# A linear-attention and ELU block on one core: the state term on four 64x64 array tiles, states without zero blocks, and a re-ordered schedule

## The chip, the core and the metric

The kernel runs on one core of one Trainium2 chip. The time is the device time of one execution in microseconds (us); the kernel before takes 214.02 us, the median of three runs (213.94 to 214.1). A profile of one execution goes with it. The engines are TensorE (PE; its weight loads are listed apart as PEld), VectorE (DVE), ScalarE (ACT), GpSimd (POOL) and the issuing queue of SyncE (SP).

## The reference

Inputs are q, k, v of shape (4, 8, 768, 64) for batch, heads, positions and head size, one decay `lam` for each head, and two weight matrices. First comes decayed linear attention, block by block, with a state of 64 x 64 for each batch and head:

```python
intra = (qb @ kb.T * Dmask) @ vb            # Dmask[i, j] = lam ** (i - j) for i >= j
inter = (qb * lam_pow) @ kv_state
out[:, :, sl] = intra + inter
kv_state = lam_block * kv_state + (kb * rev_pow).T @ vb
```

The heads are put side by side, so x has 3072 rows (batch x position) of 512. Then two dense layers with an ELU between them:

```python
h = x @ w_in                                # (3072, 512) @ (512, 2048)
g = where(h > 0, h, exp(min(h, 0)) - 1)
return g @ w_out                            # (3072, 2048) @ (2048, 512), float32
```

## The kernel before, in words

**Groups.** A block is 128 positions here. A group g is one block of one batch: g = 4 * block + batch, 24 groups. Groups 0 to 3 are worked on singly, the others in pairs (4:5, 6:7, ... 22:23); all operands of the matmuls are fp16.

**Attention of a group.** Loads of q, k, v are issued on POOL (`emit_load`, line 107) and cast on the way. `T` puts q and k in transposed form, head pairs on 128 partitions: on TensorE for groups 0 to 7 (line 285), by a transposing DMA on SP for the others (`W`, line 270). `S` makes the scores of eight heads (line 304), `att_E` multiplies them by the decay mask on VectorE into `pp` (line 320). `P` adds up the output, transposed (line 340: v times `pp`; line 346: state times q, from the second block on), and one VectorE or ScalarE instruction moves it to `xt` (lines 361 and 363; from group 8 on it also multiplies by the row decay `qs`). `kd` is k times its decay (POOL, line 176); `U` multiplies it with v for the new state (lines 408 and 417); `M` decays the old state into `stt` (line 390 on POOL; line 383 on ScalarE from group 12 on); line 440 on VectorE adds the two.

**State with zero blocks.** The state of a batch is a tile of 128 partitions, four head pairs and 128 columns. The two heads of a pair lie on the diagonal, the other two 64 x 64 blocks are zero (filled at the start, lines 202 and 718). So a state matmul contracts over 128 partitions, half of them zeros, and writes 64 output rows; `P` writes the two halves of the output rows by two matmuls beside each other.

**Burst.** From group 4 on, `B:P4:P5:U4:U5` puts the output of a pair and its two state updates behind each other on TensorE.

**Dense layers.** A unit `1:g:j` (`mm1`, line 674) makes 512 columns of h in one PSUM bank out of two (`psH`); ScalarE then runs exp and relu (lines 680, 681) and VectorE the ELU's last step (`g` or `gg`, line 640), which frees the bank. `2:g:j` (`mm2`, line 699) multiplies four tiles of g by w_out. For the pairs listed in `SEVEN` the second layer takes seven products `7:g:0` to `7:g:6` of half the columns (line 551) in place of eight; it needs sums of g (`P`, `D`, `E`: `fp`, `fd`, `fe`, lines 497 on POOL and 500 on VectorE; `SHARED` says which are on POOL) and of w_out (`wf`, line 517; token `F` on VectorE, `G` on POOL). Corners are put together by ScalarE copies, POOL and VectorE (lines 558 to 605), and stored from SP.

**Order.** Every engine runs its instructions in the order in which the program emits them. That order is written out: `POOL_ORDER` for the loads and early POOL work, `OPEN` for the opening up to unit 1:6:5, and from there one loop that puts after each unit one item of the second layer and the attention steps due there, at the distances of `AT` (units before the pair's first). So in the steady part a pair has the order

```
1:14:0 1:14:1 S16:17 7:12:0 1:14:2 7:12:1 1:14:3 B:P16:P17:U16:U17 W18 7:12:2
1:14:4 7:12:3 1:14:5 W19 Lq20 7:12:4 1:14:6 Lk20 7:12:5 1:14:7 Lv20 7:12:6
```

and the kernel ends with 1:22:7 7:20:6 7:22:0 ... 7:22:6. `BANKS` names PSUM banks for the early steps; `late` is a list of VectorE and ScalarE steps that are emitted one at a time.

Of the kernel before, what the change touches and what calls it, by code (L numbers as in the profile page):

```python
# [15 lines left out]
def kernel(  # L16
# [27 lines left out]
    WI = [2] * 8  # L44
    WO = [2] * 8
    POOL_ORDER = (
        "q1 k0 iota k2 k1 q2 v0 v1 i0 i1 v2 i3 i2 o0 o1 d0 k3 q3 i4 i5 d1 o2 d2 o3 d3 o4 v3 o5 "
        "i6 i7 k4 o7 o6 q4 k6 m4 v4 q6 d5 d4 q8 q10 k8 d6 v6 v8 d7 v10 k10 m6"
# [4 lines left out]
        "z3 z0 z1 Z2 Z1 z2 Z0 T0 T1 S0 S1 T2 P0 P1 S2 1:0:0 U0 1:1:0 P2 1:1:1 1:2:0 2:0:0 "  # L53
        "1:2:1 2:1:0 1:0:1 T3 2:2:0 1:0:2 S3 1:2:2 2:2:1 U1 1:1:2 2:1:1 2:0:1 P3 2:0:2 1:3:0 "
        "2:1:2 1:1:3 M 1:2:3 Z3 2:2:2 1:3:2 U2 1:3:1 2:1:3 1:0:3 T4 T5 2:2:3 1:3:3 S4:5 2:3:0 "
        "2:0:3 2:3:2 U3 F0 B:P4:P5:U4:U5 M 2:3:3 1:4:1 T6 1:4:0 G3 T7 2:3:1 G4 W9 1:4:3 G5 G1 "
        "S6:7 1:4:2 G2 2:5:0 2:4:0 1:4:4 1:4:5 W8 B:P6:P7:U6:U7 1:4:7 1:6:1 2:5:1 2:4:1 G7 "
        "1:4:6 1:6:0 G6 2:4:2 S8:9 1:6:2 1:6:4 2:5:2 2:5:3 W11 1:6:3 1:6:6 B:P8:P9:U8:U9 1:6:7 "
        "2:4:3 1:6:5 W10 L12"
# [4 lines left out]
    DELAY = 0  # L64
    COMB = nc.gpsimd

    SEVEN = (8, 10, 12, 14, 16, 18, 20, 22)
    SHARED = {8: 'D', 10: 'ED', 12: 'ED', 14: 'ED', 16: '', 18: '', 20: '', 22: 'ED'}
    AT = {'L': -19, 'l': 1, 'W': -13, 'T': -5, 'S': -7, 'B': -5}
    BANKS = (  # L70
        "S0=M0,A S1=D,C S2=D,M1 S3=D,B P0=M1 P1=M0 P2=B P3=A U0=B U1=B U2=B U3=M1 T0=M1,D "
        "T1=D,C T2=M0,D T3=B T4=B T5=D T6=M1 T7=D M2=C M3=M0"
# [19 lines left out]

    stp = [
        [cpool.tile([128, 2, NHP, 128], FP16, name=f"st{x}_{i}") for i in range(2)]
# [5 lines left out]
    def emit_load(w, g0):  # L100
        n = size_of[g0]
        c, b = divmod(g0, B)
        x = {"q": q, "k": k, "v": v}[w]
        src = x[b : b + n, :, c * L : (c + 1) * L].rearrange("b h p d -> p (b h) d")
        t = asb.tile([128, n, H, 64], FP16, tag=f"{w}n{n}", name=f"{w}n{g0}", bufs=4)
        {"q": qg, "k": kg, "v": vg}[w][g0] = t
        nc.gpsimd.dma_start(out=t[:].rearrange("p b h d -> p (b h) d"), in_=src)  # L107
# [38 lines left out]
    def emit_wi(i):  # L146
        written.add(("i", i))
        f0 = sum(WI[:i]) * 128
        nc.gpsimd.dma_start(
            out=wi16[i][:],  # L150
            in_=moe_w_in[:, f0 : f0 + WI[i] * 128].rearrange("(k p) f -> p k f", p=128),
        )
# [48 lines left out]
    def zero_st1(b):  # L201
        nc.vector.memset(st[b][1], 0.0)

# [8 lines left out]

    dn = cpool.tile([128, H], FP32, name="dn")
    mask = cpool.tile([128, H, 128], FP32, name="mask")
    qs = cpool.tile([128, NHP, 128], FP32, name="qs")
    ks = cpool.tile([128, H], FP32, name="ks")
# [11 lines left out]
    for hh in range(2):  # L228
        r = slice(hh * 64, (hh + 1) * 64)
        nc.vector.tensor_copy(loglam_p[r, :], loglam[r, hh::2])  # L230
    nc.vector.tensor_scalar_add(pos[:, 2:3], pos[:, 1:2], float(L))

    def emit_qs():
        for hp in range(NHP):
            nc.scalar.activation(
                qs[:, hp, :], row[:], AF.Exp, scale=loglam_p[:, hp : hp + 1]
            )
# [90 lines left out]

    def att_P(g):
        cb, b = divmod(g, B)  # L330
        until(E_done, g)
        if cb > 0:
            until(Y_done, g - B)
        vt = of(vg, g)
        qt, _ = qkT[g]
        po = bank(f"P{g}", 0, [128, NHP, 128], FP32, f"psO{g}")
        R = [slice(0, 64), slice(64, 128)]
        for hp in range(NHP):
            for hh, r in enumerate(R):
                nc.tensor.matmul(  # L340
                    po[r, hp, :], lhsT=vt[:, 2 * hp + hh, :], rhs=Pt[(g, hh)][:, hp, :],
                    start=True, stop=(cb == 0), skip_group_check=True,
                )
            if cb > 0:
                for r in R:
                    nc.tensor.matmul(  # L346
                        po[r, hp, :], lhsT=st[b][cb % 2][:, hp, r], rhs=qt[:, hp, :],
                        start=False, stop=True, skip_group_check=True,
                    )

        def evacuate():
            g0 = GFIRST[g]
            n = GSIZE[g0]
            if g0 not in xg:
                xg[g0] = asb.tile(
                    [128, NHP, n * 128], FP16, tag=f"xt{n}", name=f"xt{g0}",
                    bufs=4 if n == 1 else 2,
                )
            dst = xg[g0][:, :, (g - g0) * 128 : (g - g0 + 1) * 128]
            if g < GPE:  # L360
                nc.scalar.copy(out=dst, in_=po[:])
            else:
                nc.vector.tensor_tensor(out=dst, in0=po[:], in1=qs[:], op=ALU.mult)
            X_done.add(g)

        return [evacuate]

    stt = {}

    def att_M(g):  # L370

        cb, b = divmod(g, B)
        if cb == NCB - 1 or b % 2:
            return
        assert {f"U{g - B}", f"U{g - B + 1}"} <= seen
        until(Y_done, g - B)
        until(Y_done, g - B + 1)
        old = stp[b // 2][cb % 2]
        tmp = asb.tile([128, 2, NHP, 128], FP32, tag="stt", name=f"stt{g}", bufs=2)
        stt[g] = tmp  # L380
        if g >= MACT:
            for hp in range(NHP):
                nc.scalar.activation(
                    tmp[:, :, hp, :], old[:, :, hp, :], AF.Copy, scale=upp[:, hp : hp + 1]
                )
            return
        for hh in range(2):
            r = slice(hh * 64, (hh + 1) * 64)
            for x in range(2):
                nc.gpsimd.tensor_tensor(  # L390
                    out=tmp[r, x, :, r], in0=old[r, x, :, r],
                    in1=upp[r].unsqueeze(2).broadcast_to([64, NHP, 64]), op=ALU.mult,
                )
# [5 lines left out]
    def att_U(g, pu=None):  # L399

        cb, b = divmod(g, B)
        if cb == NCB - 1:
            return []
        vt = of(vg, g)
        if pu is None:
            full = bank(f"U{g}", 0, [128, NHP, 128], FP32, f"psU{g}")
            for hp in range(NHP):
                nc.tensor.matmul(
                    full[:, hp, :].rearrange("p (h e) -> p h e", h=2),
                    lhsT=kds[g][:, 2 * hp : 2 * hp + 2, :],  # L410
                    rhs=vt[:, 2 * hp : 2 * hp + 2, :], start=True, stop=True,
                )
        else:
            for hp in range(NHP):
                for hh in range(2):
                    r = slice(hh * 64, (hh + 1) * 64)
                    nc.tensor.matmul(
                        pu[r, hp, :], lhsT=kds[g][:, 2 * hp + hh, :], rhs=vt[:, 2 * hp + hh, :],
                        start=True, stop=True, skip_group_check=True,
                    )  # L420
        if cb > 0:
            return []
        new = st[b][1]

        def update(hh):
            r = slice(hh * 64, (hh + 1) * 64)
            nc.vector.tensor_copy(new[r, :, r], full[r, :, r])
            if hh == 1:
                Y_done.add(g)

        return [lambda: update(0), lambda: update(1)]

    def updates(g, pu):
# [4 lines left out]
        def update(hh):  # L438
            r = slice(hh * 64, (hh + 1) * 64)
            nc.vector.tensor_tensor(  # L440
                out=new[r, :, :, r], in0=stt[g][r, :, :, r], in1=pu[r], op=ALU.add
            )
            if hh == 1:
                Y_done.update((g, g + 1))

        return [lambda: update(0), lambda: update(1)]

    def burst(*ops):

        us = [int(o[1:]) for o in ops if o[0] == "U" and int(o[1:]) // B < NCB - 1]  # L450
        evs, i = [], 0
        for o in ops:
            if o[0] == "P":
                evs += att_P(int(o[1:]))
# [262 lines left out]
    def zero_st(b):  # L717
        nc.scalar.memzero(st[b][0])

# [8 lines left out]
    def ready(t):  # L728
# [4 lines left out]
        if t[0] == "U" and g < 2 * B:  # L733
            assert f"{'z' if g < B else 'Z'}{g % B}" in seen
# [4 lines left out]
    def run(t):  # L739
# [11 lines left out]
        if w in "PUzZ":  # L751
            ready(t)
        if w == "S":
# [4 lines left out]
            late.pop(0)()  # L758
            late.pop(0)()
# [6 lines left out]
        else:  # L766
            {"T": att_T_pe, "1": mm1, "2": mm2, "Z": zero_st, "z": zero_st1,
             "q": lambda g, e: cast_raw(g, "q", e), "k": lambda g, e: cast_raw(g, "k", e),
             "7": mm2_seven, "F": w_sums, "G": lambda i: w_sums(i, nc.gpsimd), "c": lambda i: (emit_qs, emit_mask, emit_ks)[i](), "W": pool_work,
# [94 lines left out]
```

## Time and profile before

| what | before |
|---|---|
| median of 3 runs | 214.02 us (213.94 to 214.1) |
| the profiled execution's own time | 213.94 us |
| span of its instructions | 212.2 us |
| TensorE busy | 196.6 us (93%) |
| POOL busy | 160.2 us (76%) |
| VectorE busy | 158.7 us (75%) |
| ScalarE busy | 138.0 us (65%) |
| unit matmuls, line 674 | 896, 101.1 us |
| score outputs, line 340 / state terms, line 346 | 192, 12.4 us / 160, 10.0 us |

The span runs from the first to the last instruction; what lies between it and the execution's own time is start and end. Busy times of matmuls overlap, so a count times a mean is more than the array's time: how often matmuls start says more. In a row of the timeline stand start, length, engine, line, operation, output and inputs, shape and count; a bracket tells how long the engine stood idle before and what ended that. In the chain of waits stand start, length and the piece of work.

### The profile page before, as it was taken

What the parts mean: (1) busy time and instruction counts of PE and PEld (TensorE: products, weight loads), DVE (VectorE), ACT (ScalarE), POOL (GpSimd) and SP (SyncE); (2) the same over time, 40 slices, a digit from 0 to 9 for tenths busy, and PEclk for the clock granted to TensorE, in tenths of its full rate; (3) what the DMA queues carried; (4) which work ended last, traced back from release to release, by engine and by line L of the source; (5) the groups of instructions that cost most, each with busy time, mean ns of one, the idle gap of its engine ahead of it and who ended that gap; (6) DMA issues with size and microseconds to landing.
All of it is one profiled execution on the core that took longest, in us unless ns stands there. A gap on an engine that the chain in (4) does not pass through costs nothing.

```text
span 212.2 us, 5654 instructions
## 1 busy us (share of the span) xinstructions
PE 196.6 (93%) x2224; PEld 157.3 (74%) x2224; DVE 158.7 (75%) x294; ACT 138.0 (65%) x277; POOL 160.2 (76%) x187
## 2 busy tenths in 40 slices
PE   0678999999999999999999999999999999999983
PEld 0457775777676776767887887888988878888862
DVE  3864482589965878889979879879989889885522
ACT  4535664874877675867866867867667667577630
POOL 7999699999999999597999999996361201206961
PEclk9999999999999999999999999999999999999999
DMA  8999999999993030999949969979999611011032
GB/s 89 132 163 192 195 188 187 161 181 191 134 180 80 3 99 5 131 165 151 125 92 154 133 83 153 163 50 151 155 81 169 103 52 50 3 51 48 3 118 79
DMA packets 102122, 24.61 MB, mean 116 GB/s; under 512 B 92624, under 2 KB 99280, under 8 KB 102096
## 3 DMA queue, kind: packets, MB, share of 16 engines
q0 software_dynamic: 79760, 13.50, 82.6%
q1 hardware_dynamic: 22336, 10.76, 26.3%
q8 instruction: 17, 0.28, 0.6%
q14 instruction: 9, 0.07, 0.1%
HBM read 27.27 MB, written 6.29 MB: 158 GB/s over the span
## 4 chain that ended last, share of the span: by engine, by line
PE 76%; ACT 7%; DVE 6%; DMA 3%; POOL 3%; issue 2%; ACTq 0%; POOLq 0%; DVEq 0%
PE psH L674 35%; PE psM L551 21%; PE psM L699 12%; DMA wi<-in_moe_w_in_dram 3%; ACT e L680 3%; ACT psH L681 3%; PE psS L304 3%; DVE gg L640 3%; PE psO L340 2%; DVE g L640 2%; PE psO L346 2%; POOL kn L107 1%; PE psT L285 1%; POOL qn L107 1%; POOL vn L107 1%
## 5 line engine op out<-in xcount | busy, mean ns | idle before, releaser
L674 PE MATMUL psH<-xt,wi 128*128 128x256 f16 (+1 forms) x896 | 101.1, 261 | 3.0 <-DVE gg L640 1.4
L674 PEld LDWEIGHTS <-wi 128*128 128x128 f16 x896 | 78.8, 99 | 18.3 <-issue 4.0
L680 ACT ACTIVATE e<-psH 128x512 f32<-128x512 f32 x96 | 57.4, 597 | 47.7 <-PE psH L674 46.6
L681 ACT ACTIVATE psH<-psH 128x512 f32<-128x512 f32 x96 | 56.9, 593 | 0.0
L640 DVE SCALAR_TENSOR_TENSOR gg<-e,psH 128x512 f16<-128x512 f32 x64 | 43.7, 683 | 16.6 <-ACT psH L681 16.3
L640 DVE SCALAR_TENSOR_TENSOR g<-e,psH 128x512 f16<-128x512 f32 x32 | 21.9, 685 | 17.3 <-ACT psH L681 17.1
L320 DVE TENSOR_TENSOR pp<-psS,mask 128x512 f16<-128x512 f32 x48 | 31.4, 683 | 4.2 <-PE psS L304 4.2
L699 PE MATMUL psM<-wo,g 128*128 128x512 f16 x128 | 31.9, 379 | 0.0
L497 POOL TENSOR_TENSOR fd<-gg 128x512 f16<-128x512 f16 x20 | 24.4, 1218 | 0.1
L176 POOL TENSOR_TENSOR kd<-kn,ks 128x512 f16<-128x512 f16 x20 | 21.0, 1054 | 4.3 <-DMA kn<-in_k_dram 4.2
L517 POOL TENSOR_TENSOR wf<-wo 128x256 f16<-128x256 f16 (+1 forms) x28 | 21.1, 794 | 0.2
L497 POOL TENSOR_TENSOR fe<-gg 128x256 f16<-128x256 f16 x16 | 11.8, 735 | 12.1 <-DVE gg L640 12.0
L594 POOL TENSOR_TENSOR t<-m,m 128x256 f32<-128x256 f32 x8 | 5.9, 737 | 18.3 <-ACT m L558 18.3
L699 PEld LDWEIGHTS <-g 128*128 128x128 f16 x128 | 11.7, 98 | 9.6
L551 PE MATMUL psM<-wf,gg 128*128 128x256 f16 x128 | 16.8, 273 | 0.8 <-DVE osb L582 0.5
L551 PE MATMUL psM<-wo,fp 128*128 128x256 f16 x128 | 16.5, 273 | 0.0
L551 PE MATMUL psM<-wf,fd 128*128 128x256 f16 x128 | 16.4, 273 | 0.0
L107 POOL DMA_DIRECT2D qn<-in_q_dram x13 | 14.8, 1136 | 0.9 <-POOLq L848 0.8
L107 POOL DMA_DIRECT2D kn<-in_k_dram x14 | 15.3, 1096 | 0.0
L107 POOL DMA_DIRECT2D vn<-in_v_dram x14 | 15.3, 1098 | 0.0
L500 DVE TENSOR_TENSOR fp<-gg 128x512 f16<-128x512 f16 x32 | 14.6, 455 | 0.6
L551 PEld LDWEIGHTS <-gg 128*128 128x128 f16 x128 | 11.9, 98 | 3.2 <-issue 0.7
(62 smaller groups left out, 249.3 us busy)
## 6 DMA issues: line engine op xcount, KB each, us to landing
out_dram<-osb SPq DMA_DIRECT2D x22, 256.0 KB, 2.7
kn<-in_k_dram POOLq DMA_DIRECT2D x10, 256.0 KB, 6.0
qn<-in_q_dram POOLq DMA_DIRECT2D x10, 256.0 KB, 6.2
vn<-in_v_dram POOLq DMA_DIRECT2D x10, 256.0 KB, 8.7
wi<-in_moe_w_in_dram POOLq DMA_DIRECT2D x8, 256.0 KB, 8.0
wo<-in_moe_w_out_dram POOLq DMA_DIRECT2D x8, 256.0 KB, 9.0
kn<-in_k_dram POOLq DMA_DIRECT2D x4, 128.0 KB, 4.2
vn<-in_v_dram POOLq DMA_DIRECT2D x4, 128.0 KB, 6.4
```

The source lines that it names most:

```text
L107: nc.gpsimd.dma_start(out=t[:].rearrange("p b h d -> p (b h) d"), in_=src)
L176: nc.gpsimd.tensor_tensor(out=kd[:], in0=of(kg, g), in1=ks[:].unsqueeze(2).broadcast_to([128, H, 64]), op=ALU.mult,)
L320: nc.vector.tensor_tensor(out=P[:], in0=pts[hh][:], in1=mask[:, hh::2, :], op=ALU.mult)
L497: nc.gpsimd.tensor_tensor(out=out[:], in0=in0, in1=in1, op=op)
L500: lambda out=out, in0=in0, in1=in1, op=op: nc.vector.tensor_tensor(out=out[:], in0=in0, in1=in1, op=op)
L517: eng.tensor_tensor(out=out, in0=in0, in1=in1, op=op)
L551: nc.tensor.matmul(out, lhsT=lhs, rhs=rhs, start=(s == 0 and m in (3, 4, 1, 7)), stop=(s == NFT // 2 - 1), skip_group_check=True,)
L640: nc.vector.scalar_tensor_tensor(out=g.rearrange("p f c t -> p (f c t)"), in0=e[:], scalar=-1.0, in1=r[:], op0=ALU.add, op1=ALU.min,)
L674: nc.tensor.matmul(pH[:, f * n * 128 : (f + 1) * n * 128], lhsT=wi16[i][:, kk, w * 128 : (w + 1) * 128], rhs=xg[g0][:, kk, :], start=(kk = ...
L680: nc.scalar.activation(e[:], pH[:], AF.Exp)
L681: nc.scalar.activation(pH[:], pH[:], AF.Relu)
L699: nc.tensor.matmul(psM[g][:, cols], lhsT=gts[(g, j * FB + f)], rhs=wo16[i][:, w, cols], start=first and f == 0, stop=end and f == FB - 1, ...
```

## The change

- **State.** A state has no zero blocks any more: 128 partitions (two heads), four head pairs, 64 columns. The zero fills go. `M` and the state update are one instruction for both halves of the partitions.
- **Output of a pair.** For groups from 4 on, `att_P2` works on both groups of a pair. The 16 state matmuls come first, each on a 64 x 64 tile of the array, in rounds of four (two row halves, two column halves); the row half decides the PSUM bank (heads of even and of odd number). The scores' matmuls follow into the same banks. Heads h and h + 4 now share the partitions of `xt`, so its row decay is a new constant `qx` (token `c3`).
- **w_in.** Its rows are loaded to match that order of heads: a load brings 64 partitions and 512 columns in place of 128 partitions and 256, so a tile is complete after two loads.
- **Schedule.** Pair 20 leaves `SEVEN`. On POOL are now P and D for pairs 8 and 16, P and E for 12 and 22, E and D for 10 and 14. `F0` becomes `G0`. `OPEN`, `POOL_ORDER`, some `BANKS` and the distances of `AT` are new: W comes two units later, the loads two units earlier. `DELAY` becomes 1, which in `flush` has the effect that 0 had.

```diff
-    WI = [2] * 8
+    WI = [4] * 4
-    OPEN = (
-        "z3 z0 z1 Z2 Z1 z2 Z0 T0 T1 S0 S1 T2 P0 P1 S2 1:0:0 U0 1:1:0 P2 1:1:1 1:2:0 2:0:0 "
-        "1:2:1 2:1:0 1:0:1 T3 2:2:0 1:0:2 S3 1:2:2 2:2:1 U1 1:1:2 2:1:1 2:0:1 P3 2:0:2 1:3:0 "
-        "2:1:2 1:1:3 M 1:2:3 Z3 2:2:2 1:3:2 U2 1:3:1 2:1:3 1:0:3 T4 T5 2:2:3 1:3:3 S4:5 2:3:0 "
...
+    OPEN = (
+        "T0 S0 T1 T2 S1 P0 S2 P1 1:0:0 1:1:0 U0 P2 1:1:1 U1 1:2:0 2:0:0 1:2:1 2:1:0 1:0:1 T3 "
+        "1:0:2 2:2:0 S3 1:2:2 2:2:1 2:0:1 P3 1:1:2 2:1:1 2:0:2 1:3:0 1:1:3 2:1:2 2:2:2 M 1:2:3 "
+        "1:3:2 U2 2:1:3 1:3:1 T4 T5 1:0:3 2:2:3 1:3:3 c3 S4:5 2:3:0 2:0:3 G0 2:3:2 U3 "
...
-    SEVEN = (8, 10, 12, 14, 16, 18, 20, 22)
-    SHARED = {8: 'D', 10: 'ED', 12: 'ED', 14: 'ED', 16: '', 18: '', 20: '', 22: 'ED'}
-    AT = {'L': -19, 'l': 1, 'W': -13, 'T': -5, 'S': -7, 'B': -5}
+    SEVEN = (8, 10, 12, 14, 16, 18, 22)
+    SHARED = {8: 'PD', 10: 'ED', 12: 'PE', 14: 'ED', 16: 'PD', 18: '', 22: 'PE'}
+    AT = {'L': -21, 'l': 1, 'W': -11, 'T': -7, 'S': -7, 'B': -5}
...
-        [cpool.tile([128, 2, NHP, 128], FP16, name=f"st{x}_{i}") for i in range(2)]
+        [cpool.tile([128, 2, NHP, 64], FP16, name=f"st{x}_{i}") for i in range(2)]
...
-            out=wi16[i][:],
-            in_=moe_w_in[:, f0 : f0 + WI[i] * 128].rearrange("(k p) f -> p k f", p=128),
+            out=wi16[i][hf * 64 : hf * 64 + 64],
+            in_=moe_w_in[r0 : r0 + 256, f0 : f0 + WI[i] * 128].rearrange(
+                "(k p) f -> p k f", p=64
+            ),
...
-                    nc.tensor.matmul(
-                        po[r, hp, :], lhsT=st[b][cb % 2][:, hp, r], rhs=qt[:, hp, :],
-                        start=False, stop=True, skip_group_check=True,
-                    )
+    def att_P2(g):
...
+        po = [bank(f"P{g + e}", 0, [128, 2, 2, 128], FP32, f"psO{g}_{e}") for e in range(2)]
+        for a in range(2):
+            for i in range(2):
+                for c in range(2):
+                    for e in range(2):
+                        nc.tensor.matmul(
+                            po[e][R[c], a, i, :],
+                            lhsT=st[(g + i) % B][cb % 2][R[e], 2 * c + a, :],
+                            rhs=qkT[g + i][0][R[e], 2 * c + a, :],
+                            start=(a + i == 0), stop=False, skip_group_check=True,
+                        )
+        for i in range(2):
+            for h in (0, 4, 1, 5, 2, 6, 3, 7):
+                scores_v(po[h % 2][R[h // 4], h % 4 // 2, i, :], g + i, h, False)
...
-        def update(hh):
-            r = slice(hh * 64, (hh + 1) * 64)
-            nc.vector.tensor_tensor(
-                out=new[r, :, :, r], in0=stt[g][r, :, :, r], in1=pu[r], op=ALU.add
-            )
+        def update():
+            nc.vector.tensor_tensor(out=new[:], in0=stt[g][:], in1=pu[:], op=ALU.add)
```

## The prediction

> **What bounds the kernel now.** I read the page first (engine rows, chain of waits), then the timeline of one steady stretch, then the few places where TensorE stands still.
>
> ```profile
> PE 196.6 (93%) x2224; PEld 157.3 (74%) x2224; DVE 158.7 (75%) x294; ACT 138.0 (65%) x277; POOL 160.2 (76%) x187
> PE 76%; ACT 7%; DVE 6%; DMA 3%; POOL 3%; issue 2%; ACTq 0%; POOLq 0%; DVEq 0%
> ```
>
> TensorE carries 76% of the chain. From about 16 us on it works nearly without a break, so a change is worth what it takes off TensorE's own sequence, plus the few holes it closes. The timeline shows what a burst costs there:
>
> ```profile
> 131.76 1.04 PE L674 MATMUL psH<-xt,wi 128*128 128x256 f16 x8
> 132.72 0.25 PE L340 MATMUL psO<-pp,vn 128*64 128x128 f16 x2
> 132.80 0.22 PE L346 MATMUL psO<-qT,st 128*64 128x128 f16 x2
> ...
> 133.64 0.42 PE L417 MATMUL psU<-vn,kd 128*64 128x64 f16 x16
> 133.99 1.05 PE L551 MATMUL psM<-wo,fp 128*128 128x256 f16 x8
> ```
>
> Blocks of eight 256-column matmuls follow each other every 0.873 us, so one takes 0.109. The eight from 131.76 fill the array until 132.63 and the burst starts at 132.72: 0.09 us lie idle where the tile form goes from 128*128 to 128*64. The burst's 16 score and 16 state matmuls run from 132.72 to 133.64, two at a time (rows of x2): 0.92 us for 16 pairs, the first a little longer, the others 0.056 apart by their starts in the trace. The state updates' eight pairs end near 133.89 and the next block starts at 133.99: again 0.10 for a change of form.
>
> ```profile
> 35.28 0.60 ACT e L680
> 36.40 0.70 DVE g L640
> 37.14 1.05 PE psH L674 x16
> ...
> 78.88 0.67 DVE st L440
> 79.59 0.53 DVE st L440
> 80.31 0.70 DVE g L640
> 81.05 1.03 PE psH L674 x8
> ```
>
> These pieces of the chain are the holes: `mm1` has two banks, and where only one other block stands between a unit's end and the unit after next, TensorE waits for ScalarE's two passes and VectorE's `g`. Before 37.14 the hole is 0.36 us, before 81.05 it is 0.30 (there because two state updates stand before `g` on VectorE). Once in each pair of groups, at its second unit, it is 0.37. The tail has two more:
>
> ```profile
> 201.33 0.93 PE L551 MATMUL psM<-wf,gg 128*128 128x256 f16 x7
> 202.58 0.28 PE L551 MATMUL psM<-wf,gg 128*128 128x256 f16 x1 [0.32 <-DVE gg L640]
> 203.37 1.03 PE L551 MATMUL psM<-wf,gg 128*128 128x256 f16 x8 [0.50 <-DVE osb L582]
> ```
>
> The first product of the last pair waits for the last `gg`; the second then waits 0.68 us (202.58 plus 0.11 to 203.37) for its bank, which the last corner of pair 20 (`osb`, line 582) still holds. The opening, last:
>
> ```profile
> 14.74 1.03 PE L674 MATMUL psH<-xt,wi 128*128 128x128 f16 x8
> 16.08 1.04 PE L674 MATMUL psH<-xt,wi 128*128 128x128 f16 x8 [0.31 <-DMA wi<-in_moe_w_in_dram]
> 17.34 1.88 PE L674 MATMUL psH<-xt,wi 128*128 128x128 f16 x16
> 19.60 1.07 PE L674 MATMUL psH<-xt,wi 128*128 128x128 f16 x16
> ```
>
> `mm1` begins when `w_in` lands: its first half on the first load, its second on the second. Sixteen matmuls take 1.88 us at 17.34 and 1.07 at 19.60: early ones run at half the pace, though the page's clock row reads 9 in every slice.
>
> **The change, part by part**, against the profiled execution: 213.94 us, a span of 212.2 and 1.74 around it, 0.08 below the median of the three runs (214.02).
>
> **State term, -1.29.** Ten bursts (P4:P5 to P22:P23) hold 16 state matmuls each: now eight pairs of 0.056, after it four rounds of four tiles. Nothing in the trace shows four tiles at once. Column halves pair (above), and the scores of line 304 show that row halves pair too: 16 of them take 0.56 us in all (128.57 to 129.13), that is 8 x 0.056 and one change of form. So a round costs between 0.056 and 0.112; I take 0.056, since in a pair the second matmul starts only 3 ns after the first. Saved: 10 x 4 x 0.056 = 2.24. But the states now stand first, in 64*64 form, and the scores follow in 128*64: one more change of form in each burst. Its price is between 0 (the column half stays 64 wide) and the 0.10 of the rows; I take 0.095, the size of every change of form at full pace: 0.95.
>
> The Trainium skill, TensorEngine Tiling (Array Packing), Tiling Modes, says that changing the mode, and not just the tile, drains the array. That speaks against the change: by the rule each burst pays as I have it; without it the gain would be 2.24. The skill's TensorE: Matmul & The Clock Gate, Part 3, lets each further tile add some 4 ns, which by an estimate would take 40 x 2 x 4 ns = 0.3 us off the gain; the trace's pairs repeat at 0.056 with no such growth.
>
> **Pair 20 leaves the seven products, +0.78 on TensorE.** Its two groups take 32 matmuls of 512 columns (line 699, four in 0.862 us): 6.90, in place of 56 of 0.109 = 6.12. In exchange, a `2:20:0` stands between the first two units of pair 22, where the order before has none, and fills the hole of 0.37. And the tail's bank: product 2 of pair 22 needs the bank of `psM21`, freed by one ScalarE copy (0.59) right behind the last unit's two passes, about 1.95 us after that unit ends on TensorE. Product 1 ends 2.23 after it (2:21:3, then the wait for `gg`, which stays). So the 0.68 goes. Next late is the P sum of pair 22, now on POOL (1.22): `gg` ends 2.07 after the unit, the sum at 3.4, and its last two factors are wanted at 3.8. It fits by 0.4; without that cover it costs what it lacks.
>
> **Order and VectorE, -0.66.** In the new order two blocks stand before the unit that waits at 37.14, so 0.36 goes. One state update of 128 partitions (0.68) replaces two of 64 partitions, so `g` at 80.31 comes 0.6 earlier and the 0.30 there goes. The other holes at second units stay. VectorE loses more (the P and E sums that go to POOL, `F0`), but it is not what ends those waits: ScalarE and TensorE are. I count 0.
>
> **Opening, +0.25.** A `w_in` load now holds all columns of four tiles for 64 partitions, so unit 1:0:0 needs both halves and can't start at 14.74. The second is the ninth POOL load in both orders, with the same bytes ahead, so it lands near 16.03 as now. Behind the waiting matmul all of TensorE queues: 1:0:0, 1:1:0, U0. Eight matmuls that ran in the hole move behind it, some 0.8 us at the slow pace; given back are U1 (0.22), now in the hole before 1:2:0, and half of that hole (0.61 now, 0.3). The loads of the next tiles (18.24, 19.55) hold later units in both. Bounds: -0.2 (they land earlier in longer rows) to +1.3, one more load of this size (16.03 less 14.69, where the two land now).
>
> **Without a price.** The zero fills (four on VectorE, 1.1; four on ScalarE, 1.4) lie before 30 us beside the wait for `w_in` or before slack. The new `qx` (four ScalarE passes, 1.3) stands behind 1:3:3; the next unit follows after S4:5, three `mm2` and a burst, 5.5 us; uncovered it costs 1.3. M on ScalarE halves its elements and moves behind 1:g:5, where the `e` of unit 6 waits some 0.6 for it; its `gg` then comes 0.1 after its bank is wanted, which the hole of the second unit behind it takes up. W goes two units later (kd, SP transposes), the loads two earlier; on SP only stores of finished corners stand ahead, and transposes landed 137.19 for scores at 144.07.
>
> Sum: -1.29 + 0.78 - 0.37 - 0.68 - 0.66 + 0.25 = -1.97, so 212.0 for this execution and 212.1 against the median.
>
> **The rivals.**
>
> **VectorE was the hidden cause** of more holes. It loses 20 P and 4 E sums (11 us at 0.455 and 0.478), eight updates (5.4) and `F0` (2.4). The kT copy that S6:7 awaits at 56.36 (hole 0.35) follows a VectorE step. If these and some half of the second-unit holes (7 x 0.37) go too, another 1.2: 210.9. Against it: the units' waits end on ScalarE.
>
> **Tiles don't overlap fourfold.** If rows and columns pair but not both, the 2.24 goes and the extra change of form stays: 214.3. Against: both kinds of pair run freely.
>
> **The opening pays in full**: 1.3, and 0.5 if TensorE's slow pace lasts longer for its later start: 213.6.
>
> **POOL becomes the bound** (the slower side). It is already full in a steady pair:
>
> ```profile
> 127.60:143.10 15.50, 15.29 (x184) 13.22 (x184) 13.05 (x24) 11.53 (x25) 15.01 (x17) 1.00 1.13 121
> ```
>
> 15.01 busy of 15.50 us. Pairs 8 and 16 gain four P sums of 1.22 (pair 16 also its four D), G0 joins (3.2); sixteen small M steps become four (-5). Between 80 and 95.6 POOL has 12.9 now and gets about 17 against 15.4 of TensorE. That backlog of 2 to 3 us stays through pair 16, since each pair brings about as much as TensorE takes. It decides where kd comes after its burst: kd(g+1) would run near 143 plus backlog, the burst is at 148.2; so from 5 us of backlog TensorE waits, every pair. If a POOL pair costs 16.8 (its sums stretch from 1.15 to 1.34 beside VectorE), five pairs bring 7 us on top of the first 2.5, less the slack of 5: 212.1 + 4.5 = 216.6.
>
> **How the numbers follow.** The sum as forecast: 0.53; VectorE 0.15; opening 0.12; no fourfold overlap 0.08; POOL 0.12. The predicted time is 212.1; the forecast alone runs from 211.4 to 213.0 (a change of form at 0 to 0.10 each, rounds of up to 0.07, opening from -0.2). The range goes to 210.9 for VectorE and to 214.3 for no overlap. A measurement here tells 0.2% (0.4 us) from no change. Faster: 0.53 + 0.15 + half of the opening + a quarter of POOL (backlog partly absorbed) = 0.77; same: the overlap case and part of the opening, 0.10; slower: the rest of POOL and of these, 0.13.
>
> **What would show it.** Right: state matmuls start in fours every 0.056, a burst is 0.13 shorter though a gap of 0.09 stands between states and scores; no wait at the second unit of pair 22 and none for `osb` in the tail; first unit near 16.1. Wrong: fours that repeat at 0.11; a pair's period that follows POOL, with PE waiting for kd or for sums; `mm1` starting past 17.

## The result, and the profile after

| what | before | after |
|---|---|---|
| median of the runs shown together | 214.06 us (213.94 to 214.34) | 220.67 us (220.22 to 222.23) |
| ratio of the two | | 1.032 (1.0268 to 1.0371) |
| the profiled execution's own time, span | 213.94, 212.2 us | 220.22, 218.5 us |

The changed kernel is 3.2% slower. Forecast were 212.1 us and a gain. Here and below a median is over all executions of a kernel in its set, while a ratio leaves out those that fell in a slower state, so the two do not always match (e2 and e12 most). The page of the changed kernel, its engine row and the shares of the chain:

```profile
PE 196.8 (90%) x2200; PEld 152.9 (70%) x2200; DVE 155.2 (71%) x253; ACT 136.0 (62%) x275; POOL 168.4 (77%) x188
PE 68%; DVE 12%; issue 6%; ACT 6%; DMA 3%; POOL 3%; DVEq 0%; ACTq 0%; POOLq 0%
```

TensorE does the same amount of work (196.8 us) in a span that is 6.3 us longer; its share of the chain falls from 76 to 68%, and VectorE's doubles. So TensorE now waits, and for VectorE. The waits of TensorE between 80 and 170 us say where, first one row of the kernel before, then two of the changed kernel (engine, line waited for: us in total, times, longest):

```profile
PE psH L674 <- DVE gg L640: 1.0, 5, 0.2
```

```profile
PE psH L718 <- DVE gg L684: 5.8, 10, 1.5
PE psO L358 <- DVE pp L336: 1.6, 3, 1.0
```

Pairs 8 to 16 lie there. From the second unit of one pair to that of the next it takes 15.41, 16.70, 17.61 and 18.69 us, where the kernel before has 15.62 and three times 15.50. Before 80 and behind 165 us the changed kernel is ahead of the kernel before, as forecast, if by less (0.32 and 0.42 for 0.50 and 0.53).

Why `gg` is late is seen one step further back, on VectorE. Its groups of corner sums by form (count | busy us, mean ns), first three of the kernel before, then three of the changed one:

```profile
L500 DVE TENSOR_TENSOR fp<-gg 128x512 f16<-128x512 f16 x32 | 14.6, 455 | 0.6
L500 DVE TENSOR_TENSOR fe<-gg 128x256 f16<-128x256 f16 x16 | 7.7, 478 | 0.0
L500 DVE TENSOR_TENSOR fd<-gg 128x512 f16<-128x512 f16 x12 | 5.0, 416 | 0.0
```

```profile
L544 DVE TENSOR_TENSOR fp<-gg 128x512 f16<-128x512 f16 x12 | 12.6, 1053 | 0.2
L544 DVE TENSOR_TENSOR fe<-gg 128x256 f16<-128x256 f16 x12 | 10.6, 887 | 0.1
L544 DVE TENSOR_TENSOR fd<-gg 128x512 f16<-128x512 f16 x12 | 8.2, 686 | 0.2
```

There are 36 of them instead of 60, and they take 31.4 us instead of 27.3. The same instruction takes 0.42 us (512 columns) or 0.285 (256) where nothing disturbs it. Here is one that is disturbed, in the timelines of VectorE, GpSimd and TensorE of the changed kernel (start, us, what):

```profile
137.34 0.68 DVE L403 TENSOR_TENSOR xt<-psO,qx 128x512 f16<-128x512 f32 x1
137.94 2.72 DVE L544 TENSOR_TENSOR fp<-gg 128x512 f16<-128x512 f16 x1
140.58 0.68 DVE L482 TENSOR_TENSOR st<-stt,psU 128x512 f16<-128x512 f32 x1
141.18 1.27 DVE L684 SCALAR_TENSOR_TENSOR gg<-e,psH 128x512 f16<-128x512 f32 x2
```

```profile
136.68 1.20 POOL L109 DMA_DIRECT2D qn<-in_q_dram  x1
137.90 0.68 POOL L541 TENSOR_TENSOR fe<-gg 128x256 f16<-128x256 f16 x1
138.53 1.16 POOL L541 TENSOR_TENSOR fd<-gg 128x512 f16<-128x512 f16 x1
139.64 0.72 POOL L649 TENSOR_TENSOR u<-t,osb 128x256 f32<-128x256 f32 x1
140.31 1.18 POOL L109 DMA_DIRECT2D kn<-in_k_dram  x1
```

```profile
139.72 1.04 PE L595 MATMUL psM<-wf,fe 128*128 128x256 f16 x8
141.91 1.03 PE L718 MATMUL psH<-xt,wi 128*128 128x256 f16 x8 [1.14 <-DVE gg L684]
```

GpSimd has issued the load of q until 137.88 and then starts `fe` at 137.90, 0.04 us ahead of VectorE's `fp`. VectorE's sum stands while `fe`, `fd` and `u` follow each other on GpSimd without a pause, and ends some 0.3 us after `u`. Below, such a sum is called held. Behind it on VectorE wait a state update and `gg`; `gg` frees the psH bank, so TensorE stands for 1.31 us at 140.6 (1.14 of them named in the row).

The kernel before has the same meeting, but it stays short, in its timelines of VectorE and GpSimd:

```profile
131.61 0.58 DVE L500 TENSOR_TENSOR fp<-gg 128x512 f16<-128x512 f16 x1
132.11 0.68 DVE L320 TENSOR_TENSOR pp<-psS,mask 128x512 f16<-128x512 f32 x1
```

```profile
131.24 0.67 POOL L497 TENSOR_TENSOR fe<-gg 128x256 f16<-128x256 f16 x1 [0.39 <-DVE gg L640]
131.87 1.34 POOL L497 TENSOR_TENSOR fd<-gg 128x512 f16<-128x512 f16 x1
```

There `fe` is 0.37 us ahead, VectorE's sum gets its turn when `fe` ends, and GpSimd's `fd` is the one that is stretched (1.34 for 1.16).

### The profile page after: what moved, and what is told of

The parts are those of the page before. It is cut to its first block, busy times and chain, and to the rows that moved or that the text cites. A ratio compares the mean times of both kernels' runs of the same rounds, so it can differ in the third digit from the quotient of the medians.

```text
span 218.5 us, 5560 instructions
## 1 busy us (share of the span) xinstructions
PE 196.8 (90%) x2200; PEld 152.9 (70%) x2200; DVE 155.2 (71%) x253; ACT 136.0 (62%) x275; POOL 168.4 (77%) x188
## 4 chain that ended last, share of the span: by engine, by line
PE 68%; DVE 12%; issue 6%; ACT 6%; DMA 3%; POOL 3%; DVEq 0%; ACTq 0%; POOLq 0%
PE psH L718 32%; PE psM L595 15%; PE psM L743 13%; DVE gg L684 5%; DMA wi<-in_moe_w_in_dram 3%; PE psO L358 3%; ACT psH L725 2%; DVE pp L336 2%; ACT e L724 2%; PE psS L320 2%; DVE fe L544 2%; POOL kn L109 1%; PE psO L388 1%; PE psU L459 1%; POOL qn L109 1%
## 5 line engine op out<-in xcount | busy, mean ns | idle before, releaser
L684 DVE SCALAR_TENSOR_TENSOR gg<-e,psH 128x512 f16<-128x512 f32 x56 | 38.0, 681 | 18.7 <-ACT psH L725 18.6
L684 DVE SCALAR_TENSOR_TENSOR g<-e,psH 128x512 f16<-128x512 f32 x40 | 27.4, 685 | 25.1 <-ACT psH L725 23.4
L743 PE MATMUL psM<-wo,g 128*128 128x512 f16 x160 | 40.1, 379 | 0.0
L541 POOL TENSOR_TENSOR fp<-gg 128x512 f16<-128x512 f16 x16 | 19.7, 1233 | 18.6 <-DVE gg L684 18.5
L561 POOL TENSOR_TENSOR wf<-wo 128x256 f16<-128x256 f16 (+1 forms) x32 | 24.1, 786 | 0.0
L743 PEld LDWEIGHTS <-g 128*128 128x128 f16 x160 | 14.9, 98 | 12.0 <-issue 0.3
L541 POOL TENSOR_TENSOR fd<-gg 128x512 f16<-128x512 f16 x16 | 19.1, 1195 | 0.0
L595 PE MATMUL psM<-wf,gg 128*128 128x256 f16 x112 | 14.6, 273 | 0.3 <-DVE gg L684 0.3
L595 PE MATMUL psM<-wo,fp 128*128 128x256 f16 x112 | 14.4, 273 | 0.0
L544 DVE TENSOR_TENSOR fp<-gg 128x512 f16<-128x512 f16 x12 | 12.6, 1053 | 0.2
```

The costliest lines, as they stand in the source:

```text
L541: nc.gpsimd.tensor_tensor(out=out[:], in0=in0, in1=in1, op=op)
L544: lambda out=out, in0=in0, in1=in1, op=op: nc.vector.tensor_tensor(out=out[:], in0=in0, in1=in1, op=op)
L561: eng.tensor_tensor(out=out, in0=in0, in1=in1, op=op)
L595: nc.tensor.matmul(out, lhsT=lhs, rhs=rhs, start=(s == 0 and m in (3, 4, 1, 7)), stop=(s == NFT // 2 - 1), skip_group_check=True,)
L684: nc.vector.scalar_tensor_tensor(out=g.rearrange("p f c t -> p (f c t)"), in0=e[:], scalar=-1.0, in1=r[:], op0=ALU.add, op1=ALU.min,)
L743: nc.tensor.matmul(psM[g][:, cols], lhsT=gts[(g, j * FB + f)], rhs=wo16[i][:, w, cols], start=first and f == 0, stop=end and f == FB - 1, ...
```

## The experiments

Three theories stood at the start: A, GpSimd has more sums (`SHARED`); B, the new distances (`AT`) put GpSimd's work beside VectorE's sums; C, the new burst, state term or bank. In the table, "lost" is worked out from the starts in each trace: the sum of TensorE's pauses of more than 0.4 us between 80 and 170 us, counted beyond the slot of the matmul ahead. The last column is span less lost.

| kernel | median us | ratio to before (interval) | span | lost (pauses) | rest |
|---|---|---|---|---|---|
| before | 214.06 | | 212.2 | 0 | 212.2 |
| changed | 220.67 | 1.032 (1.027 to 1.037) | 218.5 | 7.6 (8) | 210.9 |
| e1 sums back | 221.24 | 1.034 (1.031 to 1.038) | 219.6 | 8.5 (8) | 211.1 |
| e2 distances back | 215.61 | 1.005 (1.001 to 1.009) | 213.7 | 1.9 (1) | 211.8 |
| e3 before, new sums | 215.94 | 1.011 (1.006 to 1.016) | 215.6 | 2.9 (1) | 212.7 |
| e4 before, new distances | 219.69 | 1.028 (1.024 to 1.033) | 217.8 | 5.3 (5) | 212.5 |
| e5 loads back | 215.72 | 1.009 (1.004 to 1.014) | 214.0 | 3.3 (3) | 210.7 |
| e6 W back | 221.55 | 1.038 (1.031 to 1.044) | 219.9 | 8.8 (7) | 211.1 |
| e7 distances and sums back | 216.91 | 1.017 (1.013 to 1.021) | 215.3 | 3.9 (2) | 211.4 |
| e8 no VectorE sums | 212.39 | 0.993 (0.991 to 0.996) | 210.5 | 0 | 210.5 |
| e9 GpSimd fills | 212.21 | 0.993 (0.989 to 0.996) | 210.2 | 0 | 210.2 |
| e13 e2 with G1 early | 214.24 | 1.003 (0.999 to 1.007) | 212.0 | 1.8 (1) | 210.2 |
| e18 e13, pair 8 on VectorE | 212.38 | 0.994 (0.990 to 0.997) | 210.3 | 0 | 210.3 |

Each ratio is against the runs of the kernel before in the same set (medians 213.28 to 214.06). In all kernels of the table that carry the changed burst the rest stays between 210.2 and 211.8 us, whatever the time; the same holds for e11 (210.6), e14 and e16 (210.4) and e17 (210.2) below, not for e12 (212.8) and e15 (213.0). The forecast's sum gave a span of 212.2 - 1.97 = 210.2.

What e12 and e15 lose beside their pauses is clock. In their traces the granted clock is 0.5 for 3.41 us, from 107.1 and from 124.1 us on, close behind pauses of 2.0 and 2.5 us; a matmul of 256 columns then takes 0.213 us in place of 0.109 (an estimate from that: 1.7 us lost). In e15's timeline of TensorE the blocks of eight that start there stand 1.7 us apart:

```profile
124.21 1.89 PE L602 MATMUL psM<-wo,fp 128*128 128x256 f16 x8
125.89 1.83 PE L725 MATMUL psH<-xt,wi 128*128 128x256 f16 x8
127.56 1.04 PE L602 MATMUL psM<-wo,fp 128*128 128x256 f16 x8
```

The trace of e3 has the same from 103.6 us on, in its pause of 2.9. A mean granted clock of 0.993 or less, which such a stretch makes, stands in all six executions of e15 and in none of the 42 of e8, e9, e10 and e18, whose traces have none of the pauses counted here. What sets it off is not shown: the traces of e6, e7 and e17 have pauses of 2.0 to 2.4 us without it.

### Undoing one part, and doing one part alone (e1 to e4)

```diff
# e1: changed kernel              # e3: kernel before, the reverse
-SHARED = {8: 'PD', 10: 'ED', 12: 'PE', 14: 'ED', 16: 'PD', 18: '', 22: 'PE'}
+SHARED = {8: 'D', 10: 'ED', 12: 'ED', 14: 'ED', 16: '', 18: '', 22: 'ED'}
# e2: changed kernel              # e4: kernel before, the reverse
-AT = {'L': -21, 'l': 1, 'W': -11, 'T': -7, 'S': -7, 'B': -5}
+AT = {'L': -19, 'l': 1, 'W': -13, 'T': -5, 'S': -7, 'B': -5}
```

> The changed kernel with the old split of the sums between POOL and VectorE (P on VectorE again in pairs 8, 12, 16, 22; D on POOL in 8 and 12, E and D in 22, none in 16); all else as changed. Theory A (POOL gets more sums, so VectorE's own sums are held up by POOL's operations, and the units behind them wait): 212 to 213.5 us, VectorE's sums back at 0.42 to 0.6 us. Theory B (the new distances of the loads, of kd and W put POOL work beside VectorE's sums): 217 to 219. Theory C (the new burst or the bank it fills is at fault): 220.

> The changed kernel with the old distances (loads at -19, W at -13); the split of the sums as changed. Theory A: 218 to 221 us, sums on VectorE still above 0.8 us each. Theory B: 212 to 214. Theory C: 220.

> The kernel before with the new split of the sums (P and D on POOL in pairs 8 and 16, P and E in 12 and 22; pair 20 keeps its seven products and its sums on VectorE), all else as before. Theory A: 218 to 221 us. Theory B: 214 to 215. Theory C: 214.

> The kernel before with the new distances (loads at -21, W at -11), all else as before. Theory A: 214 to 214.5 us. Theory B: 217 to 219, with VectorE's sums near 1 us. Theory C: 214.

The distances account for most: taking them back saves 5.1 us (220.67 to 215.61), putting them into the kernel before costs 5.9 (219.69, against 213.83 for the kernel before in the same set). The times of e1, e2 and e4 lie above the ranges that B gave (e1: 221.24 for 217 to 219; e4: 219.69 for 217 to 219; e2: 215.61 for 212 to 214), and what e2 keeps is not from the distances. The sums alone cost the kernel before 2.1, in one pause of 2.9 us behind a sum of 3.89 us; taking them back out of the changed kernel saves nothing. C falls: the old kernel with the new distances loses its time in the same way, and without the new burst.

### Loads or W (e5, e6), and both parts back (e7)

```diff
# e5
-AT = {'L': -21, 'l': 1, 'W': -11, ...
+AT = {'L': -19, 'l': 1, 'W': -11, ...
# e6
+AT = {'L': -21, 'l': 1, 'W': -13, ...
# e7: SHARED as in e1 and AT as in e2 together
```

> Changed kernel with only the loads of the next pair (L, the q, k and v transfers that GpSimd and SyncE issue) put back to their place of before; the W step stays two units later. Theory B1 (the q transfer's issue on GpSimd at unit 2 delays its sums so that they start together with VectorE's): the 2.7 us sum in the middle of each pair (the one at 137.94 us in the changed kernel) goes, the one at the end of the pair stays, 217.0 to 218.5 us. Theory B2 (the W step, with GpSimd's gate-sum work right ahead of its sums of the next pair, does it all): no change, 219.5 to 221. If the loads do it all: 215 to 216.

> Changed kernel with only the W step put back to its place of before; the loads stay two units earlier. Theory B1: the 2.7 us sum in the middle of the pair stays, the one at the end of the pair goes, 217.5 to 219.5 us. Theory B2: as the changed kernel with all distances back, 215 to 216 us. If the loads alone do it: 219.5 to 221.

> Changed kernel with both the sum placement and all distances (loads, W and transposes) of before: what stays of the change is the state term on the 64x64 tiles, the bank per head parity, the grouping of w_in and the states without zero blocks. Theory: those parts are worth what was forecast (10 bursts, the tail's bank wait, the hole) and the loss is all in the placing of the loads and the sums: 211.8 to 213.2 us, ahead of both kernels. If the burst parts cost something that the loads only hid: 214 or more.

In the changed kernel the loads' two units are worth 5 us, W nothing; three pauses stay in e5. But e7, which has both the old sums and the old distances, takes 216.91 and not the 211.8 to 213.2 expected: two long sums (2.79 us at 84.8, 3.47 at 117.6) cost it 3.9. So these are not prices that add up. Each arrangement decides anew which of VectorE's sums meets which operations of GpSimd.

### Is it the shared reading? (e8, e9)

```diff
# e8: VectorE's sums left out; the products read the gate product gg instead, GpSimd's sums stay
# e9: GpSimd's sums become fills, VectorE's sums stay
-                nc.gpsimd.tensor_tensor(out=out[:], in0=in0, in1=in1, op=op)
+                nc.gpsimd.memset(out[:], 0.5)
```

> Changed kernel whose VectorE corner sums are left out: the products that read them read the gate product in their place (the result is not the reference's), GpSimd's sums and all steps stay where they are. If VectorE's sums, held beside GpSimd's work, are what makes the psH bank late, the TensorE gaps of 0.5 to 1.7 us in pairs 8 to 16 go and the time is 210.5 to 213. If it is GpSimd that is late with its own sums or with the gate sums, the time stays at 218 to 221.

> Changed kernel in which each of GpSimd's corner sums is a fill of the same tile with a constant, which reads nothing (the result is not the reference's); VectorE's sums stay. If two engines reading from SBUF at once is the cause, most of VectorE's sums take 0.42 us again (those beside u, kd and the gate sums are still held) and the time is 211 to 214. If the cause is the order on VectorE itself or anything else that GpSimd's reading has no part in, the time stays at 218 to 221.

Either one takes all eight pauses away. In e8 GpSimd has all its sums and steps at their places and TensorE waits for none of them, so GpSimd was not late. In e9 VectorE has all its sums, and its groups show what they cost beside an engine that reads nothing for its sums:

```profile
L544 DVE TENSOR_TENSOR fp<-gg 128x512 f16<-128x512 f16 x12 | 5.4, 448 | 0.2
L544 DVE TENSOR_TENSOR fd<-gg 128x512 f16<-128x512 f16 x12 | 5.0, 420 | 0.2
L544 DVE TENSOR_TENSOR fe<-gg 128x256 f16<-128x256 f16 x12 | 3.6, 301 | 0.1
```

14.0 us in place of 31.4. A caution: the fills are also shorter (0.53 us for 1.2), so e9 alone does not part reading from being busy; with e8 it shows that it takes both engines' sums at once.

The Trainium skill, SBUF — State Buffer, "SBUF: two separate sides", describes this: VectorE with two SBUF inputs and a GpSimd operation that reads SBUF share a port pair as an exclusive lock, and the one that comes second is blocked for the whole instruction of the other. The runs agree on who blocks whom (`gg` and `pp`, with one input from PSUM, keep their 0.68 us in the changed kernel) and differ on the length: the sum above stood through three instructions of GpSimd, the one of 3.89 us in e3 through four.

### Phase, or too early? (e12)

```diff
-AT = {'L': -21, ...
+AT = {'L': -27, ...
```

> Changed kernel with the loads 27 units ahead instead of 21, that is in the phase of before (19) but a whole pair (8 units) earlier; W and sums as changed. Theory of the phase (what counts is beside which of VectorE's sums GpSimd is busy issuing the transfers): as with 19, 215.2 to 216.5 us. If loads that start earlier are bad in themselves (buffers, DMA traffic): 219.5 us or more.

219.72 us over four executions; the ratio (1.020, 1.015 to 1.026) rests on two of them, at 216.92 and 218.49 us. These lie between the two expectations, so the time decides neither for a phase rule nor for early loads being bad in themselves. In the trace (of 220.94 us) long sums stand at other places (3.35 us at 88.8, 3.12 at 102.2, 2.92 at 157.2), and what stands behind TensorE's five pauses is again a held sum.

### Fewer sums on GpSimd (e11)

```diff
-SHARED = {8: 'PD', 10: 'ED', 12: 'PE', 14: 'ED', 16: 'PD', 18: '', 22: 'PE'}
-AT = {'L': -21, ...
+SHARED = {8: 'D', 10: 'D', 12: 'D', 14: 'D', 16: 'D', 18: '', 22: 'D'}
+AT = {'L': -19, ...
```

> Changed kernel with the loads at their place of before, and in every pair only the difference sum on GpSimd, both others on VectorE: GpSimd has 1.0 us per unit less to do, VectorE 0.4 us more. Theory of the shared access: fewer GpSimd operations for VectorE's sums to lose against, no sum above 1.4 us, 211.8 to 213.5 us. If VectorE, 85% busy there, is too full for it: 215 to 218.

222.9 us (ratio 1.043, 1.039 to 1.047), the worst of all, and beyond even the second branch (215 to 218). The windows row of this kernel (window, then us, and busy us by engine: PE, PEld, DVE, ACT, POOL) shows a full VectorE:

```profile
97.00:162.00 65.00, 57.77 (x691) 47.69 (x691) 64.76 (x96) 40.11 (x87) 44.13 (x43) 1.00 1.13 106
```

VectorE is "busy" for 64.76 of 65 us, but a good part is waiting inside the sums: pairs 10 to 14 each have an `fe` of 2.33 and one of 1.86 us, both begun while GpSimd issues a load, with `fd` right behind it.

### What makes a hold long (e13 to e16)

The long holds all lie beside GpSimd operations that follow each other directly, so the next theory was the backlog. Step G1 puts four weight sums on GpSimd, in the changed order right ahead of pair 8; and a small fill that reads nothing might open a door between two of the others.

```diff
# e13 (on e2) and e16 (on e5): G1 back behind G5
-S6:7 G2 W8 G5 1:4:4        ... 1:6:6 G1 1:6:3
+S6:7 G2 W8 G5 G1 1:4:4     ... 1:6:6 1:6:3
# e14 (changed kernel) and e15 (on e13): behind each GpSimd corner sum and kd
+    nc.gpsimd.memset(t[:], 0.0)        # t: 128 x 2
```

> New sum placement with the distances of before (the kernel that took 215.61 us and had one TensorE gap left, 1.9 us, behind a VectorE sum held 3.2 us beside wf, fp, fd and kd on GpSimd), and step G1, which puts four weight sums on GpSimd right ahead of pair 8, moved back to behind G5 as in the kernel before. Theory of the backlog (a VectorE sum loses to as many GpSimd operations as are queued back to back): the 3.2 us sum at pair 8 and its gap go, 213.2 to 214.3 us, no slower than the kernel before. If GpSimd's backlog there is not the cause: 215 to 216.5.

> Changed kernel with the loads and step G1 as in the kernel before, W and transposes as changed (without G1's move: 215.72 us, gaps of 1.1 us at pair 8, 1.5 at pair 10 and 0.6 at pair 14). Theory of the backlog: the gap at pair 8 goes, the others, which have other operations queued, stay or shift: 214 to 215.2 us. Otherwise 215.4 to 216.5.

> Changed kernel with a fill of two numbers (reads nothing) on GpSimd behind each of its corner sums and each kd, so that no two of those that read SBUF follow each other directly. If a VectorE sum is held until GpSimd has a moment without an operation that reads SBUF: no sum is held beyond the end of one of these (1.25 us at most beside them; the fp that is held 2.7 us beside fe, fd and u comes free after fe), and the time falls to 213 to 217 us. If GpSimd keeps the right to read through its queue whatever lies between: 220 to 222, a little more than the changed kernel.

> The first kernel of this set with the fills of the second: if both theories hold, no VectorE sum above 1.3 us and 212.5 to 214 us, ahead of the kernel before; if only the backlog counts, as the first of this set.

e13: 214.24 us, level with the kernel before. The hold at pair 8's first unit shrinks from 3.22 to 0.87 us, but one of 3.28 us comes at its second (88.02), beside `fp`, `fd` and `kd`; its pause of 1.8 us is all that is lost. e16: 215.99 (ratio 1.011, 1.007 to 1.014), nothing gained on e5: the hold at pair 8 stays (2.47 us at 84.05, now beside the state product, `kd` and `fp`), so G1 itself was not the cause there. e14: 219.02 (1.023, 1.020 to 1.027), e15: 222.79 (1.040, 1.035 to 1.045). The fills do not end a hold; in e14 three pauses of 1.6 to 1.8 us are left, behind sums of 2.8 to 3.2 us, and one of 0.4. In all six executions of e15 the clock was lower too, as said above, so not all of its time is holds. The longest of all is in e15, in the timelines of VectorE and GpSimd:

```profile
89.09 4.95 DVE L551 TENSOR_TENSOR fe<-gg 128x256 f16<-128x256 f16 x1
93.96 0.68 DVE L488 TENSOR_TENSOR st<-stt,psU 128x512 f16<-128x512 f32 x1
```

```profile
89.52 1.03 POOL L189 TENSOR_TENSOR kd<-kn,ks 128x512 f16<-128x512 f16 x1
90.50 0.09 POOL L182 MEMSET gapt<- 128x2 f32 x1
90.56 1.14 POOL L547 TENSOR_TENSOR fp<-gg 128x512 f16<-128x512 f16 x1
91.65 0.09 POOL L182 MEMSET gapt<- 128x2 f32 x1
91.71 1.14 POOL L547 TENSOR_TENSOR fd<-gg 128x512 f16<-128x512 f16 x1
92.80 0.09 POOL L182 MEMSET gapt<- 128x2 f32 x1
92.85 1.03 POOL L189 TENSOR_TENSOR kd<-kn,ks 128x512 f16<-128x512 f16 x1
93.83 0.09 POOL L182 MEMSET gapt<- 128x2 f32 x1
93.87 1.21 POOL L109 DMA_DIRECT2D qn<-in_q_dram  x1
```

A sum that needs 0.285 us stands through four operations of GpSimd (and the end of a fifth) with a fill between each two, and comes free when GpSimd turns to issuing a load. Why some sums come free at the first boundary (the 0.58 us one above) and others at the second to fifth, the runs do not settle. What the long ones share is several GpSimd operations queued in a row; not every sum beside such a row is held.

### Taking one side away where it still costs (e17, e18)

```diff
# on e13; e17, then e18
-SHARED = {8: 'PD', ...
+SHARED = {8: 'PED', ...
+SHARED = {8: '', ...
```

> The kernel with the distances and G1 of before and the new sums (214.24 us; one TensorE gap left, 1.8 us at 90.5 us, behind a VectorE sum of pair 8 held 3.28 us beside fp, fd and kd), with all three corner sums of pair 8 on GpSimd, so that VectorE has none there to be held: the gap goes, GpSimd has 0.67 us more in each of four units. Theory of the held sum: 212.2 to 213.2 us, ahead of both kernels. If GpSimd is then late with its own sums or the held sum moves to the next pair: 214 to 216.

> The same kernel with all three corner sums of pair 8 on VectorE, so that GpSimd has less to hold them with there: VectorE has 0.84 us more in each of four units, and its sums meet only kd, the transfers' issue and the state product. Theory: long holds need several GpSimd operations in a row, which are then missing: 212.2 to 213.5 us. If single ones (kd, the issue) already cost TensorE: 214 to 216.

e17: 215.16 us (1.004, 1.001 to 1.007). Pair 8 has no pause, and two stand in pair 10 (held sums of 3.15 and 2.43 us) behind GpSimd's longer queue. e18: **212.38 us, ratio 0.9935 (0.9904 to 0.9967)**, faster than both kernels. With less on GpSimd in pair 8, no sum in the whole kernel takes more than 1.07 us, and TensorE's waits between 80 and 170 us are down to this:

```profile
PE psH L718 <- DVE gg L684: 1.1, 5, 0.2
```

Those are the second units' holes, which the kernel before has too (1.0, 5, 0.2). What sets e18 apart from e13 is one line; that long holds need a queue on GpSimd is what its expectation said, and it came out.

### The state term's price alone (e10), without a verdict

```diff
# on e9
-        for a in range(2):
-            for i in range(2):
-                for c in range(2):
-                    for e in range(2):
+        for e in range(2):
+            for a in range(2):
+                for i in range(2):
+                    for c in range(2):
```

> The kernel with GpSimd's sums as fills (212.21 us), in which the state term's loops are turned so that the two row halves follow each other and no longer alternate: only the two column halves stand side by side, as in the kernel before (output not the reference's, as there). Forecast's price: 4 x 0.056 us more in each of 10 bursts, 2.2 us, so 214.4 us. If alternating the row halves brings nothing: 212.2.

213.3 us, ratio 0.999 (0.996 to 1.001), and span 210.9 for 210.2, of which 0.6 had already gone before pair 8, in the opening. The edit missed its aim: in TensorE's order `psO_0` and `psO_1` still alternate, the state matmuls start in twos, two of them in every 0.056 us, instead of fours every 0.056, and a burst is 0.02 longer. Four tiles at once were not undone, so this run does not price them; the rows of the burst below do.

## Why the prediction was wrong, step by step

**The step that failed: "the loads two earlier", under "Without a price", and with it the "I count 0" for VectorE.** The first was tested for SyncE's queue and for the landing of the data, and never for GpSimd, which issues the loads at 1.2 us each in between its sums. In the changed kernel this alone is worth 5 us (e5: 215.72); the pauses left there, 3.3 us, are gone only when W, G1 and the sums of pair 8 are placed anew too (e18). The price is no delay of GpSimd. It comes from where GpSimd's chains of sums then stand beside VectorE's. And VectorE was to have 11 us less to do and to end none of TensorE's waits: its 36 sums took 4.1 us more than the 60 before, and `gg` or `pp` behind them ended all eight pauses.

**The view that would have told.** The prediction took "11 us at 0.455 and 0.478" as VectorE's rates. The rows above of the kernel before show that `fe`, with 256 columns, took longer on average (478 ns) than `fd` with 512 (416): a mean that no work explains. It also noted that GpSimd's sums stretch "from 1.15 to 1.34 beside VectorE". Both sides of the contention stood in the profile, and neither was followed to what queues behind a held sum: `gg` and the psH bank.

**The rival "POOL becomes the bound"** had the engine, the pairs (8 to 16) and the direction, with less than half the loss (216.6), but another mechanism: `kd` or sums that come late. No wait for them appears, and e8, with the same GpSimd work, runs in 212.39. It was given 0.12.

**What held.** With the holds gone (e18), the forecast's sum can be read stretch by stretch, by the starts of pair 8's first unit and of the second units of pairs 10 and 18:

| stretch | before | e18 | difference | forecast |
|---|---|---|---|---|
| start to pair 8 | 79.02 | 78.45 | -0.57 | -0.50 (three bursts, 0.36, opening) |
| pair 8 | 17.47 | 17.08 | -0.39 | -0.43 (a burst, 0.30) |
| pairs 10 to 16 | 62.12 | 61.60 | -0.52 | -0.52 (four bursts) |
| pair 18 to the end | 53.59 | 53.17 | -0.42 | -0.53 (two bursts, pair 20, hole, bank) |

In all -1.90 for a forecast of -1.97. That it is so close is in part luck, as a finer cut shows. Ahead of unit 1:4:1 both kernels run the same matmuls; it starts at 51.30 before and at 51.35 in e18, where the terms said 0.24 earlier (opening +0.25, hole -0.36, burst -0.13). The hole is gone and a burst brings 0.10, so the opening cost some 0.5, twice its term. From there to pair 8 e18 gains 0.62, where two bursts were to bring 0.26: the hole of 0.35 at 56.36, which the prediction left to a rival, is gone too, and one of 0.28 at 63.57 is halved. Pairs 10 to 16 gain 0.10 in each period, not 0.13, and 0.12 more in pair 10 (15.40 for 15.62), which no term had.

The changed kernel itself gains 0.32 up to pair 8 (78.70) and 0.42 behind 165.33; all of its loss lies between. A burst of it on TensorE's timeline:

```profile
101.29 0.82 PE L718 MATMUL psH<-xt,wi 128*128 128x256 f16 x6
102.04 0.42 PE L388 MATMUL psO<-qT,st 64*64 64x128 f16 x16
102.39 0.64 PE L358 MATMUL psO<-pp,vn 128*64 128x128 f16 x16
102.86 0.42 PE L459 MATMUL psU<-vn,kd 128*64 128x64 f16 x16
103.21 1.05 PE L595 MATMUL psM<-wo,fp 128*128 128x256 f16 x8
```

The sixteen state matmuls start in fours, the second 0.080 us behind the first and the others 0.056 apart, so the rival without fourfold overlap is out. From block to block (102.04 to 103.21) it takes 1.17 us, before 1.27 (132.72 to 133.99). That is 0.10 saved and not 0.13: the first round in a new form lasts some 0.08, and there is one more form. The change of form after the states costs about 0.09, as priced; the pair's period in e18 is 15.40 for 15.50.

The first unit starts at 16.19 (forecast near 16.1), as the first row of the changed kernel's TensorE timeline below shows. The tail's second wait, for `osb`, is gone, and only the one for `gg` is left:

```profile
16.19 3.59 PE L718 MATMUL psH<-xt,wi 128*128 128x128 f16 x32 [0.61 <-DMA wi<-in_moe_w_in_dram]
...
208.28 0.93 PE L595 MATMUL psM<-wf,gg 128*128 128x256 f16 x7
209.54 1.16 PE L595 MATMUL psM<-wf,gg 128*128 128x256 f16 x9 [0.33 <-DVE gg L684]
```

So the sum on TensorE came out within 0.1 us, by errors that cancel, and held sums, which no step of the forecast priced, cost 7.6 us, nearly four times what all the terms together gained.

## What to carry to other kernels

An edit that only moves steps on GpSimd can cost more than one that changes TensorE's work: list what VectorE reads from SBUF with two inputs, what GpSimd queues beside it, and what stands in order behind the VectorE instruction. Look for the same instruction with a mean that its size does not explain; compare its shortest with its mean before using either as a price. When putting single edits back gives prices that do not add up, take away one side of the suspected meeting altogether (here the sums of one engine): that settled in two runs what seven rearrangements could not.

## What the runs showed that was not expected

- A VectorE sum of two SBUF operands can stand through several GpSimd operations in a row: 2.7 us beside three, 3.89 in e3 beside four, 4.95 in e15, for 0.285 to 0.42 us of work. It then ends 0.15 us (256 columns) or 0.28 to 0.29 (512) after a GpSimd operation's end, in most cases.
- A GpSimd fill of 0.09 us between two operations gives it no turn (e15), and holds can also begin while GpSimd issues a load (e11). Most sums that begin there are not held: of 112 in all traces with 0.3 us or more of such an issue still ahead, 98 take less than 0.5 us.
- In the traces of e3, e12 and e15 the granted clock falls to 0.5 for 3.41 us, in a pause of TensorE of 2.0 to 2.9 us or close behind it; that the pause sets it off is not shown.
- GpSimd's own sums lose little: 1.39 us for 1.16 at most beside one of VectorE's.
